# k and q of the last three spans: transposed by TensorE, or by transposing transfers on SyncE's queue

## Chip, cores and metric

The kernel runs on one NeuronCore of a Trainium2 chip. The metric is device time in microseconds of one launch; the median of three runs of the kernel before is 141.66 us (141.6 to 142.08).

## What is computed

A gated linear recurrence over 768 steps for 4 batches and 8 heads with head size 48, followed by a feed-forward layer with a maximum of two branches:

```
f = 1 / (1 + exp(-f_logit))
for t in range(S):
    state = f[:, :, t, :, None] * state + einsum('bhd,bhe->bhde', k[:, :, t], v[:, :, t])
    y[:, :, t] = einsum('bhd,bhde->bhe', q[:, :, t], state)
x = y as 3072 rows of 384 (all heads side by side)
g = maximum(x @ w1, x @ w2)        # d_ff = 1024
out = g @ w_out
```

## The kernel before

The sequence is cut into windows of 256 steps (W), and a window of one batch is a *span*: 3 windows by 4 batches make 12 spans, 0 to 11, and span s goes on from the state of span s - 4. In a span, partition p holds the two neighbouring steps 2p and 2p + 1 ("two", also called the parity), and the 128 partitions are two halves (h) of 64, each a chunk of 128 steps. The steps of a span, by their letters in the order:

- Lf, Lk, Lq, Lv (line 115) load f, k, q, v from SyncE, 384 KB each; E, F, G (ScalarE), e and C (a triangular matmul, line 261), X and Z (ScalarE) make the running sums of log f and their exponentials; i and j multiply the gates into k and q.
- K (line 291) and Q (line 294) write k and q, scaled by the exponentials, as bf16 into the padded tiles kp and qp: 128 partitions, 2 parities, 8 heads of 64 columns (48 used). There are three buffers of each. V packs v as bf16.
- t and u are the transposes: `transposes(s, 0, b)` for kp, `transposes(s, 1, b)` for qp (line 320). Each is 16 matmuls against an identity, one for each pair of heads (NP = 4), parity and half. They write bf16 into the banks b and b + 1, and U copies both banks (128 x 2048) into the tile `trs`, on ScalarE or VectorE (line 104). `trs` has three buffers.
- A (line 337, two parts) multiplies transposed k and q to the score matrix; m masks it on VectorE (line 345) into at_m. S (line 367) multiplies the state before by the transposed q; y (line 387) adds the masked scores times v. z is a short read that makes VectorE wait for y.
- D (line 401) makes the new state from k and v, n and N (lines 413, 418) add it in and scale.
- H and Y turn the result into xT, in bf16, transposed for the feed-forward layer.

The feed-forward layer of span g is d (line 445: xT by the difference w1 - w2, four parts of 12 matmuls each), r (a relu into gT, ScalarE line 452 or VectorE line 454), o (lines 460 and 463: 3 matmuls of xT with w2 w_out and 8 of gT with w_out, for each parity), b (copy out of PSUM) and O (stores, line 481, two transfers each). For the last span P, B and R do the same in halves. The letter w begins the steps that prepare the weights.

All of it is one list written out by hand, `ORDER` (lines 20 to 56): a word is a step, its span and part, its engine (a, v, p, s) and its PSUM bank. The program is issued in this order, so each engine and SyncE's queue carries out its own words in this order, and waits at a word until that word's data are there. Loads (L) and stores (O) share SyncE's queue. Toward the end of the list the loads end with Lv10, the stores O5 and O6 follow, and the transposes of spans 9, 10 and 11 stand together (u10 t9 u9 t10 t11 u11) between the d steps of spans 7 and 8 and o8.0. The products follow in the order A9, A11.0, A10, A11.1.

Of the kernel before, what the change touches and what calls it, by code (L numbers as in the profile page):

```python
# [12 lines left out]
BF16 = mybir.dt.bfloat16  # L13
# [6 lines left out]
ORDER = """  # L20
# [24 lines left out]
A7.0@0 b5.0a@7 D8@2 A7.1@3 F11a n8.0v S7@5 m7.0v@0 o6.0@7 Lk10s@10 F10a e11p G10a z7v@5 N8.0p  # L45
m7.1v@3 Lv10s@12 e10p C11@0 b6.0a@7 S8@1 i9v A8.1@3 V9p o5.1@7 z8v@1 m8.1v@3 K9v C10@3 y7 Z10a
b5.1v@7 D9@4 H7a@5 j11v y8 O5s Z11a Y7v@5 o6.1@7 X11a Q11p H8a@1 n9.0v Y8v@1 d7.0@4 b6.1a@7 i10p
G11a d7.1@5 O6s i11v d8.0@6 r7.0a@4 Q10v d8.1@7 N9.0v X10a d8.2@0 V10a K10v d8.3@1 r8.0a@6 K11v
d7.2@2 d7.3@3 r8.1v@0 u10@4 r7.1a@2 t9@6 u9@6 t10@4 t11@0 U9a@6 U10v@4 u11@0 o8.0@2 U11v@0 A9.0@3
b8.0a@2 S9@0 m9.0v@3 A9.1@6 D10@2 o7.1@5 z9v@0 m9.1v@6 V11v A11.0@3 y9 n10.0v D11@6 o7.0@2 n11.0v  # L50
m11.0v@3 N11.0p H9v@0 o8.1@3 b7.0v@2 N10.0v b7.1a@5 Y9v@0 O7s A10.0@4 b8.1a@3 S10@6 m10.0v@4
A10.1@0 d9.0@2 z10v@6 d9.1@3 m10.1v@0 d9.2@4 r9.0a@2 d9.3@5 A11.1@0 r9.1a@4 S11@2 y10 z11v@2
m11.1v@0 o9.0@4 H10a@6 Y10v@6 y11 b9.0a@4 d10.0@0 H11v@2 d10.1@1 d10.2@4 r10.0v@0 o9.1@6 Y11v@2
d10.3@5 d11.0@0 r10.1a@4 d11.1@1 b9.1a@6 d11.2@2 O9s d11.3@3 O8s o10.0@4 r11.1v@2 r11.0v@0 o10.1@3
o11.0@0 b10.0a@4 b10.1a@3 O10s P11.0@1 b11.0a@0 O11s P11.1@0 B11.0v@1 R11.0s B11.1a@0 R11.1s
"""


@with_exitstack
def kernel(  # L60
# [16 lines left out]
    C = 128  # L77
    HC = C // 2
    W = 2 * C
    nw = S // W  # L80
    NP = H // 2
# [10 lines left out]
    work = ctx.enter_context(tc.tile_pool(name="work", bufs=2))  # L92
# [8 lines left out]
    engines = {"a": nc.scalar, "v": nc.vector, "p": nc.gpsimd, "s": nc.sync}  # L101

    def copy(e, out, in_):
        (nc.scalar.copy if e == "a" else engines[e].tensor_copy)(out, in_)  # L104
# [7 lines left out]
    def load(nm, s, e, slot):  # L112
        w, b = divmod(s, B)
        src = sources[nm][b, :, w * W:(w + 1) * W, :].rearrange("h (p two) d -> p h (two d)", two=2)
        engines[e].dma_start(out=slots[:, slot, :].rearrange("p (h x) -> p h x", h=H), in_=src)  # L115
        loaded[s][nm] = slots[:, slot, :].rearrange("p (h two d) -> p h two d", h=H, two=2)

    def staged(i, a):
        return slots[:, 4 * i:4 * i + 4, :].rearrange("p s x -> p (s x)").rearrange("p (a x) -> p a x", a=a)
# [3 lines left out]
    def load_columns(dst, w, e, h):  # L123
        cols = slice(h * d_ff // 2, (h + 1) * d_ff // 2)
        engines[e].dma_start(out=dst[:, :, cols], in_=w.rearrange("(k p) m -> p k m", p=C)[:, :, cols])

    def load_wo(e, h):
        part = slice(h * FG // 2, (h + 1) * FG // 2)
        engines[e].dma_start(out=wo_f[:, part, :],
                             in_=moe_w_out.rearrange("(j p) m -> p j m", p=C)[:, part, :])  # L130
# [13 lines left out]
    for h in range(2):  # L144
        rows = slice(h * HC, (h + 1) * HC)
# [3 lines left out]
    for nm, n_bufs, shape in (("e", 2, [C, H, DP]), ("kp", 3, [C, 2, H, DP]),  # L149
                              ("qp", 3, [C, 2, H, DP]), ("vb", 4, [C, 2 * H * DP + 2 * GAP])):  # L150
        padded[nm] = []
        for i in range(n_bufs):
            t = consts.tile(shape, BF16, name=f"{nm}{i}")
# [9 lines left out]
    def pad(nm, s):  # L163
        if s not in holders[nm]:
            holders[nm].append(s)
        return padded[nm][holders[nm].index(s) % len(padded[nm])]
# [75 lines left out]
    gate, ell, one, cum, inv, dec, tr, at_b, at, states, sadd, tmps = ({} for _ in range(12))  # L242

    def step_E(s):
        gate[s] = work.tile([C, H, 2, D], F32, name="gate", tag="gate", bufs=2)
        nc.scalar.activation(flat(gate[s]), flat(loaded[s]["f"]), AF.Exp, bias=0.0, scale=-1.0)  # L246

    def step_F(s):
        ell[s] = work.tile([C, H, 2, D], F32, name="ell", tag="ell", bufs=2)
        nc.scalar.activation(flat(ell[s]), flat(gate[s]), AF.Ln, bias=1.0, scale=1.0)  # L250

    def step_G(s):
        one[s] = work.tile([C, H, D], F32, name="one", tag="one", bufs=2)
        nc.scalar.activation(one[s], ell[s][:, :, 1, :], AF.Exp, bias=0.0, scale=-1.0)

    def step_e(s, e):
        engines[e].tensor_add(pad("e", s)[:, :, 0:D], ell[s][:, :, 0, :], ell[s][:, :, 1, :])  # L257

    def step_C(s, b):
        ps, t = banks[:, b, :], pad("e", s)  # L260
        nc.tensor.matmul(out=ps[:, 0:HD].rearrange("p (h d) -> p h d", h=H), lhsT=u_inc,  # L261
                         rhs=t[:, :, 0:D], start=True, stop=True)
        for j in range(NP):
            nc.tensor.matmul(out=ps[:, HD + 2 * j:HD + 2 * j + 2],
                             lhsT=t[:, 2 * j:2 * j + 2, :].rearrange("p h e -> p (h e)"),
                             rhs=ones2, start=False, stop=True, skip_group_check=True)
        cum[s] = ps
# [56 lines left out]
    def step_U(s, e, b):  # L324
        t = work.tile([C, 2, 2, NP, 2, HC], BF16, name="trs", tag="trs", bufs=3)
        copy(e, t.rearrange("p h x j a t -> p h (x j a t)"), banks16[:, b:b + 2, :])
        tr[s] = t

    def step_A(s, jj, b):
        t = tr[s]  # L330
        for j in range(2 * jj, 2 * jj + 2):
            for par in range(2):
                for h in range(2):
                    for r in range(2):
                        rows = slice(r * DP, r * DP + D)
                        ps = banks[:, b + r, :].rearrange("p (j a t) -> p j a t", j=2, a=2)
                        nc.tensor.matmul(out=ps[h * HC:(h + 1) * HC, j % 2, par, :],  # L337
                                         lhsT=t[rows, h, 0, j, par, :],
                                         rhs=t[rows, h, 1, j].rearrange("p a t -> p (a t)"),
                                         start=True, stop=True, skip_group_check=True)  # L340

    def step_m(s, jj, b):
        if jj == 0:
            at[s] = work.tile([C, 2, 2, 2, 2, C], BF16, name="at_m", tag="at_m", bufs=2)
        nc.vector.tensor_mul(at[s][:, jj].rearrange("p r j a t -> p (r j) (a t)"),  # L345
                             banks[:, b:b + 2, :].rearrange("p r (j x) -> p (r j) x", j=2),
                             mask_f.unsqueeze(1).to_broadcast([C, 4, 2 * C]))
# [3 lines left out]
    def has_state(s, h):  # L351
        return s >= B or h > 0

    def state_before(s, h):
        return states[s][:, 0] if h else states[s - B][:, 1]

    def step_S(s, b):
        t = tr[s]
        ys[s] = [banks[:, b + h, :].rearrange("p (j t) -> p j t", j=NP) for h in range(2)]
        for h in range(2):  # L360
            if not has_state(s, h):
                continue
            st = state_before(s, h)
            for j in range(NP):
                for r in range(2):
                    rows = slice(r * DP, r * DP + D)
                    nc.tensor.matmul(  # L367
                        out=ys[s][h][r * DP:(r + 1) * DP, j, :], lhsT=st[rows, j, :],
                        rhs=t[rows, h, 1, j].rearrange("p a t -> p (a t)"),
                        start=(j == 0), stop=False, skip_group_check=True)  # L370


# [176 lines left out]
    def store_wd(part, e, b):  # L549
# [3 lines left out]

    steps = {
        "Lf": lambda s, e, b: load("f", s, e, b), "Lk": lambda s, e, b: load("k", s, e, b),
        "Lq": lambda s, e, b: load("q", s, e, b), "Lv": lambda s, e, b: load("v", s, e, b),
        "Wa": lambda i, e, b: load_columns(w1_f, moe_w1, e, i),
        "Wb": lambda i, e, b: load_columns(w2_f, moe_w2, e, i),
        "Wo": lambda h, e, b: load_wo(e, h),
        "E": lambda s, e, b: step_E(s), "F": lambda s, e, b: step_F(s), "G": lambda s, e, b: step_G(s),  # L560
        "e": lambda s, e, b: step_e(s, e), "C": lambda s, e, b: step_C(s, b),
        "X": lambda s, e, b: step_X(s), "Z": lambda s, e, b: step_Z(s),
        "i": lambda s, e, b: step_i(s, e), "j": lambda s, e, b: step_j(s, e),
        "K": lambda s, e, b: step_K(s, e), "Q": lambda s, e, b: step_Q(s, e),
        "V": lambda s, e, b: step_V(s, e),
        "t": lambda s, e, b: transposes(s, 0, b), "u": lambda s, e, b: transposes(s, 1, b),
        "U": lambda s, e, b: step_U(s, e, b),
        "A": lambda s, i, e, b: step_A(s, i, b), "m": lambda s, i, e, b: step_m(s, i, b),
        "S": lambda s, e, b: step_S(s, b), "y": lambda s, e, b: step_y(s),
        "z": lambda s, e, b: step_z(s, b),  # L570
        "H": lambda s, e, b: step_H(s, e, b), "Y": lambda s, e, b: step_Y(s, e, b),
# [9 lines left out]
        "ws": lambda i, e, b: subtract(i, e), "wp": lambda i, e, b: permuted(i, b),  # L581
        "we": lambda i, e, b: store_wd(i, e, b),
    }
    for word in ORDER.split():
        key, of, e, b = re.fullmatch(r"([A-Za-z]+)([0-9.]+)([avps]?)@?([0-9]*)", word).groups()
        steps[key](*map(int, of.split(".")), e, int(b or 0))


# [28 lines left out]
```

## Time and profile before

| | |
|---|---|
| median of three runs | 141.66 us |
| the profiled execution, device time | 142.46 us |
| its span in the trace | 140.7 us |
| granted clock of TensorE | 1.0 throughout |
| busy: TensorE matmuls / weight loads | 121.1 us (86%) / 90.0 us (64%) |
| busy: VectorE / ScalarE / GpSimd | 110.0 us (78%) / 87.5 us (62%) / 47.0 us (33%) |
| transposes, line 320, all spans | 384 matmuls, a record of one 190 ns |
| copies of trs | 7 on VectorE, mean 1218 ns; 5 on ScalarE, mean 1863 ns |
| DMA | 28.66 MB, mean 204 GB/s; no bytes to speak of from 104 to 107.4 us |

The profile is one execution. Matmuls overlap: the record of one is longer than its step, so a group's cost on the path is read from the chain of work that ended last, which follows the program back from its last instruction to what released each step. Times in all views are microseconds from the span's start. The "xN" behind a line is the number of instructions merged into it.

### The profile page before, as it was taken

To read this page: it belongs to the slowest core of one execution; us is meant where nothing else is said; L and a number is where in the kernel's file an instruction comes from. 1 tells how busy PE (TensorE), PEld (TensorE's weight loads), DVE (VectorE), ACT (ScalarE), POOL (GpSimd) and SP (SyncE) were. 2 spreads that over 40 slices of the span, in tenths; PEclk is the share of its full clock that TensorE was granted. 3 is DMA by queue.
4 is the path that set the end of the run, shared out by engine and by line. 5 is a ranking of instruction groups with operands and counts; after the bars stand their busy time and mean duration, and the time that the engine had idled before them with its cause. 6 is when DMAs were issued, how large, how long until landed. Compare 5 with 4: busy or idle time off the path is not lost.

```text
span 140.7 us, 5377 instructions
## 1 busy us (share of the span) xinstructions
PE 121.1 (86%) x2331; PEld 90.0 (64%) x2331; DVE 110.0 (78%) x196; ACT 87.5 (62%) x145; POOL 47.0 (33%) x68
## 2 busy tenths in 40 slices
PE   0033799896999999999899999997999999999990
PEld 0023679654866786868566786675886668678670
DVE  5666799896879997999979898899688895770510
ACT  3624889569988899499774999724884114303120
POOL 7444205405194536800692842529100100000000
PEclk9999999999999999999999999999999999999999
DMA  4999999999999999999999899999400012000754
GB/s 104 272 329 342 388 281 312 340 241 249 272 262 264 266 267 271 221 275 235 240 277 240 204 259 261 257 224 290 112 13 5 5 40 72 7 0 18 211 125 99
DMA packets 56248, 28.66 MB, mean 204 GB/s; under 512 B 50464, under 2 KB 54688, under 8 KB 56224
## 3 DMA queue, kind: packets, MB, share of 16 engines
q1 hardware_dynamic: 56064, 28.22, 79.3%
q8 instruction: 18, 0.29, 0.9%
q10 hardware_dynamic: 160, 0.10, 0.3%
q14 instruction: 6, 0.05, 0.1%
HBM read 23.59 MB, written 4.72 MB: 201 GB/s over the span
## 4 chain that ended last, share of the span: by engine, by line
PE 49%; DMA 13%; DVE 10%; SPq 8%; issue 6%; POOL 6%; ACT 5%; ACTq 0%; DVEq 0%; POOLq 0%
PE banks L463 16%; PE banks L445 11%; DMA slots<-in_v_dram 8%; PE banks L460 7%; SPq L115 6%; DMA slots<-in_q_dram 4%; POOL vb L104 4%; PE banks L337 4%; PE banks L320 3%; DVE wdn L536 2%; PE banks L387 2%; PE banks L367 2%; PE banks L401 2%; SPq L481 2%; DVE at_m L345 2%
## 5 line engine op out<-in xcount | busy, mean ns | idle before, releaser
L463 PE MATMUL banks<-wo,gT 128*128 128x384 bf16 x184 | 33.7, 326 | 0.0
L445 PE MATMUL banks<-xT,wd 128*128 128x256 bf16 x288 | 33.6, 273 | 0.0
L345 DVE TENSOR_TENSOR at_m<-banks,mask 128x1024 bf16<-128x1024 f32 x24 | 29.1, 1217 | 1.8 <-PE banks L337 1.6
L445 PEld LDWEIGHTS <-wd 128*128 128x128 bf16 x288 | 27.3, 98 | 3.8
L452 ACT ACTIVATE gT<-banks 128x1024 bf16<-128x1024 f32 x18 | 18.4, 1032 | 11.6 <-PE banks L445 11.4
L463 PEld LDWEIGHTS <-gT 128*128 128x128 bf16 x184 | 18.0, 98 | 11.9
L104 ACT COPY ob<-banks 128x384 f32<-128x384 f32 (+1 forms) x19 | 8.9, 468 | 20.1 <-PE banks L463 15.2
L433 DVE SCALAR_TENSOR_TENSOR xT<-tail,gaps,banks 128x256 bf16<-128x256 bf16 x36 | 15.1, 474 | 0.1
L460 PE MATMUL banks<-m,xT 128*128 128x384 bf16 x69 | 15.1, 328 | 0.0
L246 ACT ACTIVATE gate<-slots 128x768 f32<-128x768 f32 x12 | 10.2, 848 | 6.9 <-DMA slots<-in_f_logit_dram 6.9
L104 POOL CAST vb<-slots 128x384 bf16<-128x384 f32 (+2 forms) x15 | 8.7, 614 | 14.2 <-DMA slots<-in_v_dram 14.2
L257 POOL TENSOR_TENSOR e<-ell 128x384 bf16<-128x384 f32 x8 | 8.0, 1001 | 13.5 <-ACT ell L250 13.5
L337 PE MATMUL banks<-trs 48*64 48x128 bf16 x384 | 10.5, 227 | 2.2 <-DVE trs L104 1.9
L418 POOL TENSOR_TENSOR state<-tmp_s,dec 128x256 bf16<-128x256 f32 x10 | 6.4, 647 | 17.8 <-DVE tmp_s L413 17.8
L261 PE MATMUL banks<-e,u_inc 128*128 128x384 bf16 x12 | 4.2, 354 | 9.1 <-DVE e L257 7.9
L454 DVE TENSOR_SCALAR gT<-banks 128x1024 bf16<-128x1024 f32 x6 | 7.2, 1219 | 4.3 <-PE banks L445 4.3
L337 PEld LDWEIGHTS <-trs 48*64 48x64 bf16 x384 | 7.5, 110 | 4.8 <-issue 2.2
L250 ACT ACTIVATE ell<-gate 128x768 f32<-128x768 f32 x12 | 10.0, 844 | 0.4
L294 POOL TENSOR_TENSOR qp<-slots,dec 128x768 bf16<-128x768 f32 x4 | 7.3, 1818 | 8.7 <-ACT inv L271 6.7
L104 ACT COPY trs<-banks 128x2048 bf16<-128x2048 bf16 x5 | 9.3, 1863 | 0.9 <-PE banks L320 0.9
L104 DVE COPY trs<-banks 128x2048 bf16<-128x2048 bf16 x7 | 8.4, 1218 | 1.5 <-PE banks L320 1.5
L291 DVE TENSOR_TENSOR kp<-slots,inv 128x768 bf16<-128x768 f32 x8 | 7.5, 954 | 1.4 <-ACT inv L271 1.2
(73 smaller groups left out, 195.2 us busy)
## 6 DMA issues: line engine op xcount, KB each, us to landing
slots<-in_f_logit_dram SPq DMA_DIRECT2D x12, 384.0 KB, 6.5
slots<-in_k_dram SPq DMA_DIRECT2D x12, 384.0 KB, 5.7
slots<-in_q_dram SPq DMA_DIRECT2D x12, 384.0 KB, 6.2
slots<-in_v_dram SPq DMA_DIRECT2D x12, 384.0 KB, 5.9
out_dram<-ob SPq DMA_DIRECT2D x22, 192.0 KB, 3.6
slots<-in_moe_w_dram SPq DMA_DIRECT2D x4, 768.0 KB, 8.4
slots<-in_moe_w_out_dram SPq DMA_DIRECT2D x2, 768.0 KB, 7.4
out_dram<-ob SPq DMA_DIRECT2D x2, 96.0 KB, 2.2
```

Source lines behind the costliest of these rows:

```text
L104: (nc.scalar.copy if e == "a" else engines[e].tensor_copy)(out, in_)
L115: engines[e].dma_start(out=slots[:, slot, :].rearrange("p (h x) -> p h x", h=H), in_=src)
L246: nc.scalar.activation(flat(gate[s]), flat(loaded[s]["f"]), AF.Exp, bias=0.0, scale=-1.0)
L250: nc.scalar.activation(flat(ell[s]), flat(gate[s]), AF.Ln, bias=1.0, scale=1.0)
L257: engines[e].tensor_add(pad("e", s)[:, :, 0:D], ell[s][:, :, 0, :], ell[s][:, :, 1, :])
L337: nc.tensor.matmul(out=ps[h * HC:(h + 1) * HC, j % 2, par, :], lhsT=t[rows, h, 0, j, par, :], rhs=t[rows, h, 1, j].rearrange("p a t -> p ( ...
L345: nc.vector.tensor_mul(at[s][:, jj].rearrange("p r j a t -> p (r j) (a t)"), banks[:, b:b + 2, :].rearrange("p r (j x) -> p (r j) x", j=2) ...
L433: engines[e].scalar_tensor_tensor(out=x[:, kt], in0=tails[s], scalar=gaps[:, kt:kt + 1], in1=ps[:, :, kt], op0=ALU.mult, op1=ALU.add)
L445: nc.tensor.matmul(out=ps[:, f, :], lhsT=wd[:, kt, ff * C:(ff + 1) * C], rhs=xT[g][:, kt, :], start=(kt == 0), stop=(kt == KT - 1))
L452: nc.scalar.activation(dst, src, AF.Relu)
L460: nc.tensor.matmul(out=ps, lhsT=xT[g][:, kt, cols], rhs=m2[:, kt, :], start=(kt == 0), stop=False)
L463: nc.tensor.matmul(out=ps, lhsT=gT[g][:, ff, cols], rhs=wo[:, ff, :], start=False, stop=(ff == FG - 1))
```

## The change

For spans 9, 10 and 11 the words t, u and U are left out of the order. In their place stand six words T on SyncE, T*s*.0 for k and T*s*.1 for q. Each is one transposing transfer of the whole padded tile (128 x 1024 bf16) from SBUF to the tile `trs` in SBUF. T9.1 and T9.0 stand behind O6; T11.1, T10.1, T10.0 and T11.0 behind K11, still ahead of all later stores. Apart from these words the order is the same. The tile of these spans is laid out by tensor, parity, pair of heads, half and step, where U's is by half, tensor, pair, parity and step; A and S read both through the same view. `FIRST` is an empty list and does nothing.

```diff
-G11a d7.1@5 O6s i11v d8.0@6 r7.0a@4 Q10v d8.1@7 N9.0v X10a d8.2@0 V10a K10v d8.3@1 r8.0a@6 K11v
-d7.2@2 d7.3@3 r8.1v@0 u10@4 r7.1a@2 t9@6 u9@6 t10@4 t11@0 U9a@6 U10v@4 u11@0 o8.0@2 U11v@0 A9.0@3
-b8.0a@2 S9@0 m9.0v@3 A9.1@6 D10@2 ...
+G11a d7.1@5 O6s T9.1s T9.0s i11v d8.0@6 r7.0a@4 Q10v d8.1@7 N9.0v X10a d8.2@0 V10a K10v d8.3@1
+r8.0a@6 K11v T11.1s T10.1s T10.0s T11.0s d7.2@2 d7.3@3 r8.1v@0 r7.1a@2 o8.0@2 A9.0@3 b8.0a@2 S9@0
+m9.0v@3 A9.1@6 D10@2 ...
...
     def step_U(s, e, b):
         t = work.tile([C, 2, 2, NP, 2, HC], BF16, name="trs", tag="trs", bufs=3)
         copy(e, t.rearrange("p h x j a t -> p h (x j a t)"), banks16[:, b:b + 2, :])
-        tr[s] = t
+        tr[s] = t.rearrange("p h x j a t -> p x h j a t")
+
+    def step_T(s, x, e):
+        if s not in tr:
+            t = work.tile([C, 2, 2, NP, 2, HC], BF16, name="trs", tag="trs", bufs=3)
+            tr[s] = t.rearrange("p h x j a t -> p (h x j a t)").rearrange(
+                "p (x a j h t) -> p x h j a t", x=2, a=2, j=NP, h=2)
+        out = tr[s][:, x].rearrange("p h j a t -> p a j h t").rearrange("p a j h t -> p (a j) (h t)")
+        engines[e].dma_start_transpose(
+            out=out, in_=pad("kpqp"[2 * x:2 * x + 2], s).rearrange("p two h e -> p (two h e)"))
...
-                                         lhsT=t[rows, h, 0, j, par, :],
-                                         rhs=t[rows, h, 1, j].rearrange("p a t -> p (a t)"),
+                                         lhsT=t[rows, 0, h, j, par, :],
+                                         rhs=t[rows, 1, h, j],
...
-                        rhs=t[rows, h, 1, j].rearrange("p a t -> p (a t)"),
+                        rhs=t[rows, 1, h, j],
...
+        "T": lambda s, x, e, b: step_T(s, x, e),
```

More of the change, by code (lines that the diff above doesn't have):

```diff
@@ L47, with words @@
 b5.1v@7 D9@4 H7a@5 j11v y8 O5s Z11a Y7v@5 o6.1@7 X11a Q11p H8a@1 n9.0v Y8v@1 d7.0@4 b6.1a@7 i10p
-G11a d7.1@5 O6s i11v d8.0@6 r7.0a@4 Q10v d8.1@7 N9.0v X10a d8.2@0 V10a K10v d8.3@1 r8.0a@6 K11v
-d7.2@2 d7.3@3 r8.1v@0 u10@4 r7.1a@2 t9@6 u9@6 t10@4 t11@0 U9a@6 U10v@4 u11@0 o8.0@2 U11v@0 A9.0@3
[L50 to L55, printed above, removed]
-"""
+G11a d7.1@5 O6s T9.1s T9.0s i11v d8.0@6 r7.0a@4 Q10v d8.1@7 N9.0v X10a d8.2@0 V10a K10v d8.3@1
+r8.0a@6 K11v T11.1s T10.1s T10.0s T11.0s d7.2@2 d7.3@3 r8.1v@0 r7.1a@2 o8.0@2 A9.0@3 b8.0a@2 S9@0
+m9.0v@3 A9.1@6 D10@2 o7.1@5 z9v@0 m9.1v@6 V11v A11.0@3 y9 n10.0v D11@6 o7.0@2 n11.0v m11.0v@3
+N11.0p H9v@0 o8.1@3 b7.0v@2 N10.0v b7.1a@5 Y9v@0 O7s A10.0@4 b8.1a@3 S10@6 m10.0v@4 A10.1@0 d9.0@2
+z10v@6 d9.1@3 m10.1v@0 d9.2@4 r9.0a@2 d9.3@5 A11.1@0 r9.1a@4 S11@2 y10 z11v@2 m11.1v@0 o9.0@4
+H10a@6 Y10v@6 y11 b9.0a@4 d10.0@0 H11v@2 d10.1@1 d10.2@4 r10.0v@0 o9.1@6 Y11v@2 d10.3@5 d11.0@0
+r10.1a@4 d11.1@1 b9.1a@6 d11.2@2 O9s d11.3@3 O8s o10.0@4 r11.1v@2 r11.0v@0 o10.1@3 o11.0@0
+b10.0a@4 b10.1a@3 O10s P11.0@1 b11.0a@0 O11s P11.1@0 B11.0v@1 R11.0s B11.1a@0 R11.1s
+"""
+FIRST = ""
+def words(order):
+    for word in order.split():
+        key, of, e, b = re.fullmatch(r"([A-Za-z]+)([0-9.]+)([avps]?)@?([0-9]*)", word).groups()
+        yield key, tuple(map(int, of.split("."))), e, int(b or 0)
 @with_exitstack
@@ L116, in load @@
         loaded[s][nm] = slots[:, slot, :].rearrange("p (h two d) -> p h two d", h=H, two=2)
+    for key, of, e, b in words(FIRST):
+        load(key[1], *of, e, b)
     def staged(i, a):
@@ L583 @@
     }
-    for word in ORDER.split():
-        key, of, e, b = re.fullmatch(r"([A-Za-z]+)([0-9.]+)([avps]?)@?([0-9]*)", word).groups()
-        steps[key](*map(int, of.split(".")), e, int(b or 0))
+    for key, of, e, b in words(ORDER):
+        steps[key](*of, e, b)
 _INS = ['q', 'k', 'v', 'f_logit', 'moe_w1', 'moe_w2', 'moe_w_out']
```

## The prediction, made before the changed kernel was run

> **What bounds the kernel now.** I read three views in this order: the page's slices, the chain of work that ended last, and the busy time by stage. The slices show which engine is full where the change lies; one slice is 3.52 us, so 100 us is the 29th.
>
> ```profile
> PE   0033799896999999999899999997999999999990
> ...
> DVE  5666799896879997999979898899688895770510
> ACT  3624889569988899499774999724884114303120
> ...
> DMA  4999999999999999999999899999400012000754
> ```
>
> TensorE is full from the tenth slice on. VectorE is nearly as full up to the 26th, and the DMA engines are busy until the 28th: up to about 98 us several things bound together. Then the loads end, and only TensorE stays full. The chain from there, in order of time (start, length, what):
>
> ```profile
> 98.74 5.24 PE banks L445 x48
> 103.98 1.51 PE banks L320 x96
> 105.49 0.59 PE banks L460 x3
> 106.08 1.30 PE banks L463 x8
> 107.38 0.35 PE banks L337 x16
> ...
> 110.53 0.35 PE banks L337 x16
> ...
> 115.26 0.35 PE banks L337 x16
> ```
>
> L320 is the transposes: 96 of them in one block, 1.51 us, all on the chain. The three L337 lines are the first products of spans 9, 11 and 10 (A9.0, A11.0, A10.0, in this order): who needs the transposed tiles, and when. The stages (PE, PEld, DVE, ACT, POOL busy, clock, DMA share, GB/s) confirm that nothing else ends late here:
>
> ```profile
> 98.70:104.00 5.30, 5.30 (x55) 4.57 (x54) 4.18 (x6) 4.13 (x8) 0.18 (x1) 1.00 0.33 80
> 104.00:105.50 1.50, 1.50 (x97) 1.45 (x97) 0.98 (x2) 1.48 (x2) 0.00 (x0) 1.00 0.00 0
> 105.50:107.40 1.90, 1.90 (x18) 1.00 (x22) 1.90 (x2) 1.30 (x1) 0.00 (x0) 1.00 0.00 0
> 107.40:115.30 7.90, 7.90 (x169) 5.30 (x173) 7.06 (x16) 0.96 (x3) 0.62 (x1) 1.00 0.02 4
> 115.30:136.10 20.80, 20.80 (x284) 15.77 (x281) 10.33 (x16) 6.21 (x10) 0.00 (x0) 1.00 0.27 67
> ```
>
> TensorE has no gap from 98.7 to 136.1, so each microsecond taken from it here reaches the end, and each microsecond of waiting put into it does too. The DMA engines are idle from 104 to 107.4.
>
> [...] after the 7.9 us of idling at the start, 32 products of L337 took 1.07 us, later 0.64.
>
> ```profile
> 14.86 1.07 PE L337 MATMUL banks<-trs 48*64 48x128 bf16 x32 [1.64 <-DVE trs L104]
> 27.51 0.64 PE L337 MATMUL banks<-trs 48*64 48x128 bf16 x32 [0.31 <-DVE trs L104]
> ```
>
> **Removed on TensorE.** Spans 9, 10, 11, two tensors, 16 transposes each: 96, the block above: -1.51 us on the chain. (Each record shows 190 ns, but they overlap to 15.7 ns per step, so a price by the single record would be twelve times too high.) What is late next: o8.0 moves from 105.49 to 103.98. It reads in its last four products what the DVE relu r8.1 writes, and that ends at 103.33 + 1.22 = 104.55; at 0.59 us for its first three products and 1.30/8 for each later one, the first of the last four starts at 103.98 + 0.59 + 4 x 0.163 = 105.22. It fits with 0.67 us to spare.
>
> **Removed copies.** One on ScalarE (1.86 us) and two on VectorE (2.36 us together), at 105 to 107.4. They stand beside the matmuls L460 and L463 and not on the chain: nothing. If TensorE stopped being the bound, they would give back at most those 2.36 us. The PSUM banks of the transposes come free earlier, which no chain entry waits for.
>
> **Changed reads.** The tile of these spans has another layout: the moving operand of A and S is two runs of 64 instead of 128 in a row. L261 reads runs of 48 with gaps and takes 326 ns for 384 columns, L460 reads 384 in a row in 330: nothing. At the worst, were each of their 144 products (32 of A and 16 of S in each span) 5 ns longer, 0.7 us.
>
> **Added on SyncE's queue.** The six transfers T9.1 T9.0 T11.1 T10.1 T10.0 T11.0 stand behind the stores of O6, the last of which issues at
>
> ```profile
> 99.93 0.60 SPq L481 DMA_DIRECT2D out_dram<-ob  x1
> ```
>
> so SyncE is free at 100.53. The sources are ready or nearly: K9, Q9 and Q11 are written by 97.92 (the last by POOL, from 96.10, 1.82), the others by VectorE:
>
> ```profile
> 100.19 0.95 DVE L294 TENSOR_TENSOR qp<-slots,dec 128x768 bf16<-128x768 f32 x1
> ...
> 101.58 1.83 DVE L291 TENSOR_TENSOR kp<-slots,inv 128x768 bf16<-128x768 f32 x2
> ```
>
> The last at 103.41, when the sixth transfer won't yet have its turn. So the queue itself sets the time. If each transfer holds it for X and the last needs L more to land, T9 is there at 100.53 + 2X + L and T11 at 100.53 + 6X + L. They are needed 1.51 earlier than the chain shows: A9.0 at 107.38 - 1.51 = 105.87, A11.0 at 110.53 - 1.51 = 109.02. A10.0 comes 4.73 us after A11.0 and finds its tile there. TensorE takes its queue in order: what is behind a waiting A11.0 (y9, D11, o7.0, o8.1) waits too.
>
> L: no store lands in less than 1.9 us after issue, with 0.5 to 0.6 of it the issue; I take 1.5.
>
> X is the one cost that this trace doesn't show. One transfer carries 128 x 1024 bf16 = 262,144 bytes in 1,024 rows of 256 bytes[...].
> - [...]
> - By rows, from this trace: a load moves 1,024 rows of 384 bytes; at the 259 GB/s of a full stage (84 to 88.3 us) that is 1.5 us.
> - [...]
> - [...]
>
> I take 2.26[...].
>
> **The sum.** T9 lands at 100.53 + 4.52 + 1.5 = 106.55, 0.68 late. T11 lands at 100.53 + 13.56 + 1.5 = 115.59, 6.57 after 109.02; this contains the 0.68. The second wait alone is 5.89 us[...], +1.7 (between 0 and 2.3; the latter from the start of this trace, where from 14.86 to 20.58, 5.7 us, products took some 40% of their time too much). Together -1.51 + 6.57 + 1.7 = +6.8. The profiled execution took 142.46 us (span 140.7, 1.76 around it) and would take 149.3; the median of the runs shown is 0.8 lower, and on it I forecast 141.66 + 6.8 = **148.4 us**. Behind the six on SyncE wait the stores of O7, due at about 111 and now issued after 114.1: their buffer is taken again only by b11.0 at the end, over 20 us later: nothing. With copies gone from VectorE nothing else stretches.
>
> **Rivals.**
> - Faster: the transfers run at the rate of copies, in the idle DMA engines after 101. The DMA share of 0.00 from 104 to 107.4 speaks for it[...]. At X = 1.0 T9 lands at 104.0 and T11 at 108.0, both in time, and the whole block is saved: 141.66 - 1.51 = 140.15. It decides this way while 6X + 1.5 stays under 109.02 - 100.53, X under 1.17; the stall has eaten the gain at X = 1.42.
> - No change: X is about 1.5, by rows. T11 lands at 111.0, 2.0 late: +0.5, 142.2 us. For it speaks that the loads of this trace are small rows throughout; against it that these rows lie in SBUF.
> - Much slower[...]. X = 3.5 puts T11 at 123.0: -1.51 + 14.0 + 1.7 = +14.2, 155.9 us. [...]
> - Other engines as the bound: VectorE is 7.06 of 7.90 us busy in the stage from 107.4, but after the change it starts this stage 2.36 us less loaded. I give it nothing.
>
> **How the numbers follow.** Fast (X up to 1.3): 0.22. Near 1.4 to 1.5: 0.11. Likeliest (1.5 to 3.5): 0.50, on its own 142.4 to 155.9. Above: 0.17. The range goes from the full gain, 140.1, to X = 3.5, 155.9, and leaves out the last case. 0.5% is 0.7 us, about what a measurement of this kernel can tell from no change: faster 0.22, same 0.11, slower 0.67.
>
> **What would show it.** No L320 between 103.9 and 105.5. Six issues on SyncE after 100.5, each 2.2 us apart: right; 0.6 apart and landing within 3 us: the fast rival. TensorE's waits before L337 of span 11 (some 6 us) and span 9 (under 1), their releaser a DMA into trs; the L463 behind them slower than 0.163 us per step for some microseconds if the clock falls. I am wrong if A11.0 starts at about 109.0, or if the transfers take over 3.5 us each.

## The result, and the profile after

| | before | after |
|---|---|---|
| median, first set (4 runs each) | 141.63 us | 143.22 us |
| ratio, 95% interval | | 1.0107 [1.0072, 1.0143] |
| again, in a later set (43 and 22 runs) | 142.18 us | 143.06 us |
| ratio, 95% interval | | 1.0046 [1.0021, 1.0072] |
| profiled execution, device time / span | 142.46 / 140.7 us | 142.89 / 141.1 us |

Medians here and below are of all executions, while the ratios leave out those more than 1.5% above the fastest of their kernel, and so can differ from the quotient of the medians.

The change makes the kernel about 1 us slower, not 6.8. The page's slices of after, TensorE and the DMA engines, show where: the row of nines now has dents in slices 30 and 32 (the one in the 27th lies ahead of the change, as the one in the 28th did before), and the DMA engines, idle there before, are busy into the 32nd.

```profile
PE   0033899997999999999999999969969699999990
...
DMA  4999999999999999999999999889699313000844
```

The chain of work that ended last, in order of time, names the two dents:

```profile
98.27 5.25 PE banks L467 x48
...
103.54 1.03 ACT gT L474
...
104.62 0.65 PE banks L482 x3
...
106.56 0.38 PE banks L359 x16
...
107.89 3.10 DMA trs<-kp
...
111.03 0.42 PE banks L359 x16
```

The block of 96 transposes behind the 48 d matmuls is gone: 1.51 us won. But o8.0 (L482) doesn't follow at 103.52. It waits until 104.62 for ScalarE's r7.1, which reads PSUM banks 2 and 3, and o8.0 writes bank 2: 1.10 us lost. A9.0 (first L359) finds its tile. A11.0 (the L359 at 111.03) waits for the sixth transfer: TensorE's waits list 1.3 us for it, and it takes nothing from behind A11.0 meanwhile (busy 0.02 us from 109.7 to 111). Along the chain that is -1.51 + 1.10 + 1.3 = +0.9. As causes the two waits don't add up, though: A11.0 starts when the sixth transfer lands, and without the wait at o8.0 it would only wait longer there (shown below by the run with another bank). From the start of the d block to A11.0 it is 111.03 - 98.27 = 12.76 us, before 110.53 - 98.74 = 11.79: +0.97. Behind A11.0 nothing changes: A10.0 follows 4.80 us later, before 4.73.

SyncE's queue (start, length) shows the six issues:

```profile
100.14 1.48 SPq L348 DMA_TRANSPOSE trs<-qp  x1
101.68 2.01 SPq L348 DMA_TRANSPOSE trs<-kp  x1
103.79 2.62 SPq L348 DMA_TRANSPOSE trs<-qp  x2
106.50 2.68 SPq L348 DMA_TRANSPOSE trs<-kp  x2
```

The last four follow each other by 1.35 to 1.39 us, each issue 1.24 to 1.30 long, where a store takes 0.60. From issue to landing it is 3.1 to 3.4 us for these four. T9.0 lands at 105.78 and T11.0 at 110.99.

### The profile page after: what moved, and what is told of

It reads as the page before. It is cut to its first block, busy times and chain, and to the rows that moved or that the text cites. A ratio compares the mean times of both kernels' runs of the same rounds, so it can differ in the third digit from the quotient of the medians.

```text
span 141.1 us, 5192 instructions
## 1 busy us (share of the span) xinstructions
PE 120.3 (85%) x2235; PEld 89.0 (63%) x2235; DVE 108.1 (77%) x194; ACT 85.9 (61%) x144; POOL 46.8 (33%) x68
## 4 chain that ended last, share of the span: by engine, by line
PE 69%; DMA 12%; DVE 6%; POOL 5%; ACT 3%; issue 2%; SPq 1%; ACTq 0%; DVEq 0%; POOLq 0%
PE banks L467 21%; PE banks L485 18%; PE banks L482 8%; DMA slots<-in_f_logit_dram 5%; PE banks L359 5%; DMA slots<-in_v_dram 4%; PE banks L409 4%; PE banks L332 3%; POOL vb L113 3%; PE banks L389 2%; PE banks L423 2%; DVE at_m L367 2%; DMA trs<-kp 2%; PE banks L566 2%; PE banks L273 1%
## 5 line engine op out<-in xcount | busy, mean ns | idle before, releaser
L482 PE MATMUL banks<-m,xT 128*128 128x384 bf16 x69 | 15.1, 327 | 1.1 <-ACT gT L474 1.1
L359 PE MATMUL banks<-trs 48*64 48x128 bf16 x384 | 10.5, 227 | 3.3 <-DVE trs L113 2.0
L113 POOL CAST vb<-slots 128x384 bf16<-128x384 f32 (+2 forms) x15 | 8.0, 571 | 14.3 <-DMA slots<-in_v_dram 14.3
L359 PEld LDWEIGHTS <-trs 48*64 48x64 bf16 x384 | 7.5, 110 | 5.9 <-DVE trs L113 2.2
L303 POOL TENSOR_TENSOR kp<-slots,inv 128x768 bf16<-128x768 f32 x4 | 7.5, 1864 | 4.1 <-DVE slots L292 4.0
L435 DVE TENSOR_TENSOR tmp_s<-banks,state 128x256 f32<-128x256 f32 x16 | 6.7, 418 | 2.7 <-PE banks L423 2.3
```

Of the source, the lines that this page charges most:

```text
L303: engines[e].tensor_mul(pad("kp", s)[:, :, :, 0:D], by_parity(loaded[s]["k"]), both(inv[s]))
L482: nc.tensor.matmul(out=ps, lhsT=xT[g][:, kt, cols], rhs=m2[:, kt, :], start=(kt == 0), stop=False)
```

## The experiments

The measure below, beside the median, is the stretch from the start of the d block to A11.0, read from each profile's chain as above (for the plain copies and merged, from TensorE's timeline). It leaves out what differs upstream from run to run: the start of the block alone lies between 97.8 and 98.8 us in all these profiles but halves (99.5). The runs come from three sets on different chips, each with its own runs of the kernel before, which is why that median changes from row to row; between sets the stretch and the ratio are the better guides.

| kernel | d block to A11.0 (us), against before | median / median of before | ratio, 95% |
|---|---|---|---|
| changed, again | 12.80, +1.01 | 143.06 / 142.18 | 1.0046 [1.0021, 1.0072] |
| bank | 12.52, +0.73 | 144.10 / 142.18 | 1.0118 [1.0065, 1.0171] |
| bank again | 12.63, +0.84 | 144.26 / 142.14 | 1.0093 [1.0058, 1.0128] |
| order | 11.46, -0.33 | 141.78 / 142.18 | 0.9970 [0.9945, 0.9994] |
| bank and order | 10.73, -1.06 | 140.84 / 142.18 | 0.9900 [0.9860, 0.9940] |
| early | 10.19, -1.60 | 140.18 / 142.21 | 0.9871 [0.9823, 0.9918] |
| early, bank 2 | 11.45, -0.34 | 141.53 / 142.14 | 0.9969 [0.9949, 0.9990] |
| merged | 10.98, -0.81 | 141.28 / 142.14 | 0.9931 [0.9905, 0.9957] |
| plain copies | 11.88, +0.09 | 141.75 / 142.21 | 0.9971 [0.9945, 0.9996] |
| a seventh | 14.36, +2.57 | 146.31 / 142.21 | 1.0272 [1.0199, 1.0344] |
| halves | 20.53, +8.74 | 153.56 / 142.21 | 1.0725 [1.0638, 1.0811] |

**The changed kernel again.**

> The changed kernel once more, on the chip of the next three. My theory: against the chain of before it loses 1.10 us where o8.0 waits for PSUM bank 2 (ScalarE relu r7.1a still reads it) and 1.47 us where A11.0 waits for the sixth transfer, and wins 1.51 us for the 96 transposes: +1.06 us, about 142.7 beside a kernel before of 141.6. Rival: a part of the slowdown (the medians differ by 1.6 us) comes from somewhere else, so the ratio is again about 1.011 while both waits are the same length as in the first trace.

Both waits are as long as at first, but the ratio is 1.0046, not 1.011 (the two intervals just meet, at 1.0072): the rival falls. The stretch says +1.0 us, this median +0.9. What the first set of four runs had beyond that didn't come again, and where it came from is not known.

**The bank alone.**

```diff
-r7.1a@2 o8.0@2 A9.0@3 b8.0a@2
+r7.1a@2 o8.0@5 A9.0@3 b8.0a@5
```

> o8.0 and its copy b8.0 use PSUM bank 5 in place of bank 2. My theory: o8.0 starts right behind the last d, 1.1 us earlier, but A11.0 then waits so much longer for the sixth transfer, which lands at the same time: 0.0 us against the changed kernel (within 0.3). Rival: the bank wait is what costs, and the end comes 1.1 us earlier.

By the trace as expected: o8.0 follows at once, TensorE then waits for transfers twice (A9.0 0.3 to 0.5 us, A11.0 1.8 to 2.1 us, over this run and its repeat), and A11.0 again starts when the sixth transfer lands:

```profile
108.09 3.13 DMA trs<-kp
...
111.27 0.42 PE banks L359 x16
```

The stretch is only 0.2 us shorter (T9.0's issue took 1.75 us in the repeat, 2.01 in the changed kernel). So in the changed kernel the bank wait costs next to nothing: the sixth transfer sets the time. But the median is 1 us *above* the changed kernel, which neither theory had. The same kernel was therefore run once more:

> The bank edit alone once more, for a narrower interval. My theory: the time of the changed kernel, 0.7 to 1.1 us over the kernel before, since A11.0 waits for the sixth transfer whatever TensorE does ahead of it. Rival (the edit itself costs something, as its median of 144.1 us could mean): 1.7 us or more over the kernel before.

The median came out high again. The granted clock of the single executions tells them apart. In 9 of these 19 its mean is 0.993 or more, and their median is 143.03 us: the changed kernel's 143.02 (20 of its 22 executions). In the other 10 it is 0.985 to 0.988, and their median is 144.6. So the edit itself costs nothing where the clock holds. That the longer pause at A11.0, 1.8 to 2.1 us instead of 1.3, more often lets the clock fall is argued from these counts, as neither profile of this kernel caught a fall; the difference, 1.6 us, is about what one fall costs under the seventh transfer, where it was caught (1.5).

**The order of the transfers.**

```diff
-T11.1s T10.1s T10.0s T11.0s
+T11.1s T11.0s T10.1s T10.0s
```

> T11.0 moved ahead of T10.1 and T10.0, nothing else. My theory: span 11's tile lands as the fourth transfer, at about 108.4, A11.0 finds it there, and 1.4 us of waiting goes; A10.0 comes after 114 and finds its tile too: -1.4 us against the changed kernel, 0.4 under the kernel before. Rival (the wait at A11.0 only shows what another limit behind it would take anyway, such as VectorE or the later stores): under 0.5 us faster than the changed kernel.

-1.3 us in both measures, against the changed kernel. The chain has no transfer left from the d block on:

```profile
98.53 5.25 PE banks L467 x48
...
103.81 1.03 ACT gT L474
...
106.83 0.35 PE banks L359 x16
...
109.99 0.35 PE banks L359 x16
```

The wait at A11.0 was real, and only the place in the queue made it. What is left of the 1.51 us is 1.51 - 1.10 = 0.4.

**Both.** The edits of bank and of order together.

> Both edits. My theory: with the sixth transfer out of the way the bank now counts, but A9.0 then meets the second transfer, which lands at about 105.8, 0.4 after it could start: -1.4 - 0.7 = -2.1 us against the changed kernel, some 1.1 under the kernel before (140.5 beside 141.6). Rival (the two waits are independent and each is worth what it shows): -2.5 us. Rival (the bank is worth nothing at all): -1.4 us.

-2.2 us against the changed kernel by the medians, -2.1 by the stretch; expected -2.1. A9.0 now waits 0.5 us for the second transfer, which lands at 106.06. So the bank, worth almost nothing alone, is worth 0.7 by the stretch once the sixth transfer is out of the way.

**Span 9's transfers earlier.** On top of both:

```diff
-O5s Z11a
+O5s T9.1s T9.0s Z11a
...
-O6s T9.1s T9.0s i11v
+O6s i11v
```

> As bank_order, and T9.1 and T9.0 moved ahead of the stores of O6, right behind those of O5. My theory: span 9's tile lands before 102 and A9.0 no longer waits for it, so the whole block of 1.51 us is saved: another 0.7 us under bank_order, about 1.5 under the kernel before (140.6 beside a before of 142.2). Rival: there the transfers meet the last load (v of span 10), V10 comes late and holds up r7.0 behind it on ScalarE; then nothing is gained or up to 1 us lost. The issue of T9.0 shows the price of issuing alone: about 1.25 us if issuing sets the rate, about 0.6 if the DMA engines do.

The fastest of all versions, 1.3% under the kernel before. The chain runs through on TensorE alone:

```profile
98.22 5.24 PE banks L467 x48
103.46 0.49 PE banks L482 x3
103.95 1.30 PE banks L485 x8
105.25 0.35 PE banks L359 x16
...
108.41 0.35 PE banks L359 x16
```

The stretch is 1.60 us shorter than before: the whole block of 1.51, and 0.10 because the first three products of o8.0 take 0.49 us right behind the d block, where they took 0.59 behind the transposes. The transfers met no load that mattered: TensorE waits for none of them. T9.1 issues at 96.0 and takes 1.38 us, T9.0 1.55: nearer the expectation's 1.25 than its 0.6, but not a clean price, as the DMA engines were busy (share 1.09 from 98.2 to 103.4 us).

**The same, with o8.0 in bank 2.** Against the version before it:

```diff
-r7.1a@2 o8.0@5 A9.0@3 b8.0a@5
+r7.1a@2 o8.0@2 A9.0@3 b8.0a@2
```

> As early, but o8.0 and b8.0 back in bank 2: the two transfers of span 9 early and T11.0 fourth, nothing else. My theory: no wait for a transfer is left, so the bank wait now counts in full: 1.1 us over early, 1.51 - 1.10 = 0.4 us under the kernel before, the same as order, where span 9 was in time as well. Rival (the bank wait only counts together with a late transfer): the time of early, 1.5 us or more under the kernel before.

It gives the stretch of order (11.45 and 11.46) and its median within 0.3 us. The bank wait counts in full as soon as no transfer is late: 1.26 us in the stretch, 1.10 of waiting and 0.16 because the first three products behind it take 0.65 us, not 0.49.

**What sets 1.36 us: halves.** Each transfer cut into two of 128 x 512:

```diff
+        for a in range(2):
+            engines[e].dma_start_transpose(
+                out=out[:, a * NP:(a + 1) * NP, :], in_=src[:, a].rearrange("p h e -> p (h e)"))
```

> Each of the six transfers cut into two of half the size, nothing else. My theory (the DMA engines are full and set 1.36 us for each 256 KB; issuing is held up by them): the same bytes take the same time, T11.0 lands within 0.5 us of where it did, and the time is that of the changed kernel within 0.5 us. Rival (issuing sets the rate[...]): a half takes 1.0 us of SyncE, the twelve end 2.8 us later, +2.8 us.

Both fell, the theory wholly, and the loss is far more than the rival's 2.8 us. SyncE's queue, twelve issues now:

```profile
101.36 4.30 SPq L350 DMA_TRANSPOSE trs<-qp  x2
105.72 2.56 SPq L350 DMA_TRANSPOSE trs<-kp  x2
108.39 5.13 SPq L350 DMA_TRANSPOSE trs<-qp  x4
113.62 5.14 SPq L350 DMA_TRANSPOSE trs<-kp  x4
```

Half the bytes in half the rows, and an issue still takes 1.20 to 1.27 us, where a whole one took 1.24 to 1.30. The stages (second-last number: DMA share) show that the engines don't hold it up:

```profile
105.00:110.00 5.00, 2.65 (x37) 1.54 (x38) 0.29 (x1) 1.26 (x2) 0.00 (x0) 1.00 0.48 96
```

So issuing a transposing transfer costs some 1.25 us of SyncE at 128 x 512 and at 128 x 1024. A price of the issue that grows with the size, on which the prediction rested, is refuted here: half the size changes it by less than 0.1 us. Of the 10.5 us over the changed kernel the stretch explains 7.8, six issues more; behind its pauses TensorE also runs at a lower clock (mean 0.966 to 0.974 in all four executions).

**Plain copies.** The six transfers without transposing; the target's rows are 144 elements apart, so that the pieces stay 256 bytes:

```diff
-            out=out, in_=pad("kpqp"[2 * x:2 * x + 2], s).rearrange("p two h e -> p (two h e)"))
...
+            t = work.tile([C, 2, 2 * NP, C + 16], BF16, name="trs", tag="trs", bufs=3)
...
+        engines[e].dma_start(
+            out=plains[s][:, x, :, 0:C],
+            in_=pad("kpqp"[2 * x:2 * x + 2], s).rearrange("p two (j r) e -> p (two j) (r e)", r=2))
```

> The six transfers are plain copies of the same bytes in the same 1,024 pieces of 256 bytes each; k and q of spans 9 to 11 are left untransposed, so part of the computation is left out. My theory (the transposing costs nothing beyond moving 1,024 small rows): SyncE's issues follow each other by 1.2 to 1.4 us as before and the wait at A11.0 stays within 0.5 us of 1.5. Rival [...]: issues follow by 0.6 to 1.1 us, the sixth lands 2 us earlier and A11.0 doesn't wait: 1.5 us under the changed kernel.

In between. A plain issue can take 0.62 us, half of a transposing one:

```profile
99.70 0.63 SPq L350 DMA_DIRECT2D trs<-qp  x1
100.38 0.85 SPq L350 DMA_DIRECT2D trs<-kp  x1
101.33 3.10 SPq L350 DMA_DIRECT2D trs<-qp  x2
104.53 1.90 SPq L350 DMA_DIRECT2D trs<-kp  x2
```

Yet the sixth lands 9.95 us after the first issue (at 109.65), in the changed kernel 10.85 (110.99). From 104.5 to 109.5 the engines are full (share 0.96) and move 206 GB/s, in the changed kernel from 104 to 110 also full (1.08) and 212 (from 104 to 109 us in 4,365 packets for 1.08 MB, some 250 bytes each). That is 262,144 bytes in 1.24 to 1.27 us: the engines have a limit of their own for such pieces, and it happens to lie at the same 1.25 us as the issue. Without transposing the sixth lands 0.9 us sooner, not 2.

**One transfer per span.** kp and qp in one tile, three transfers (T9.0, T11.0, T10.0) of 512 KB, with the edits of bank and order.

```diff
+        kq.append(consts.tile([C, 2, 2, H, DP], BF16, name=f"kq{i}"))
+    padded["kp"], padded["qp"] = [t[:, 0] for t in kq], [t[:, 1] for t in kq]
...
+        engines[e].dma_start_transpose(
+            out=whole[s].rearrange("p (b t) -> p b t", t=C),
+            in_=kq[at_s].rearrange("p x two h e -> p (x two h e)"))
```

> kp and qp of a span lie side by side in one tile, so that each span is one transposing transfer of 512 KB: T9, T11, T10, with the bank edit. If an issue costs 1.25 us whatever its size and nothing else limits: three issues of about 1.3 us, T11 lands near 106, A9.0 finds its tile, and the time is that of early. If the 16 DMA engines limit (1.25 us for each 1,024 pieces of 256 bytes, as in plain): the issues stretch to about 2.5 us, T9 lands at 105.5 to 106 as in bank_order and T11 at 108.4, and the time is that of bank_order, 0.5 to 0.7 us over early. [...]

The second case, the engines' limit. T9 waits long behind the stores, the other two read:

```profile
103.99 1.91 SPq L357 DMA_TRANSPOSE trs<-kq  x1
105.98 2.18 SPq L357 DMA_TRANSPOSE trs<-kq  x1
```

They land at 108.4 and 110.8: 2.4 us for 512 KB, so again 1.2 for 256 KB. The stretch is 0.25 us longer than with bank and order. Half as many issues bring nothing, because the engines were already full (from 104 to 110 us they move 224 GB/s, in the changed kernel 212).

**A seventh transfer.** One more ahead of T11.0, into a tile that nobody reads.

```diff
-K11v T11.1s T10.1s T10.0s T11.0s
+K11v T11.1s T10.1s T10.0s M10.0s T11.0s
```

> One more transposing transfer (k of span 10 again, into a tile that nobody reads) ahead of T11.0. My theory: T11.0 lands one interval later and A11.0 waits 1.2 to 1.4 us longer: +1.3 us against the changed kernel. Rival (the wait at A11.0 isn't set by the place in the queue): under 0.4 us.

Against the changed kernel the stretch is 1.6 us longer (1.42 of it one more interval: T11.0 issues at 109.62, 1.42 after the transfer ahead of it). The median rose by 3.25. The stages (TensorE busy first, granted clock third from the end) show the other half:

```profile
109.80:112.90 3.10, 0.19 (x2) 0.00 (x1) 0.87 (x4) 0.48 (x1) 0.00 (x0) 0.99 0.79 148
112.90:117.40 4.50, 4.50 (x76) 3.21 (x77) 1.89 (x3) 0.00 (x0) 0.62 (x1) 0.63 0.02 4
117.40:120.00 2.60, 2.60 (x58) 1.74 (x57) 2.39 (x6) 0.48 (x1) 0.00 (x0) 1.00 0.24 51
```

After 2.9 us of waiting the granted clock is 0.63 over the next 4.5 us (the 32 products of y9 take 1.07 us by record, in the changed kernel 0.62), and 1.00 again from 117.4. A11.0, y9, D11 and o7.0 take 112.90 to 117.42 where the changed kernel takes 111.03 to 114.04: 4.52 against 3.01, +1.5 us.

## Why the prediction was wrong, by its steps

- **The bound and the gain.** Right. From 98.7 us TensorE alone sets the end, the block is worth 1.51 us, and early gets it back whole (-1.60 in the stretch). The copies and the changed reads were worth nothing, as said: 16 products of A take 0.42 us by record in both layouts.
- **"It fits with 0.67 us to spare."** Wrong, and missed by asking only what o8.0 *reads*. It also writes PSUM bank 2, which r7.1 on ScalarE still read until 104.57. The transposes had covered that wait, and the trace of before had it to read: r7.1 ended there at 104.02 + 1.02 = 105.04, 1.06 us behind the 103.98 at which the prediction started o8.0.

```profile
104.02 1.02 ACT L452 ACTIVATE gT<-banks 128x1024 bf16<-128x1024 f32 x1 [0.70 <-PE banks L445]
```

In the changed kernel this miss cost next to nothing (bank, -0.2 in the stretch). It counts once the transfers are in time: bank and order against order alone, -0.73; early against early with bank 2, -1.26.
- **"I take 2.26."** This is the step that failed: the mechanism, a queue of six whose last holds up A11.0, was right, but its price was not. X is 1.36 us, so 6 x 0.90 = 5.4 us of the forecast delay never came, and with it the slower clock that hung on the long wait. 2.26 was my estimate, a price of the issue that grows with the size, which no trace had shown; measured, the issue is some 1.25 us, at half the size too. And the 16 engines needed 1.2 to 1.27 us for 256 KB in pieces of 256 bytes, transposed or not. The estimate by rows from this trace's own loads, 1.5, was the nearest, and I had passed over it. Transposing ran at nearly the rate of copying (10.85 against 9.95 us for the six), and with the engines full that rate was 206 to 212 GB/s.
- **L.** 1.5 was low: from the end of the issue to the landing of T11.0 it was 110.99 - 109.19 = 1.8.
- **The queue as the cause of the wait.** Right: with T11.0 fourth, no wait for a transfer is left (order), with one more ahead the wait grows by 1.6 us, 1.42 of it one interval (seventh). With X = 1.36 and L = 1.8 the prediction's own formula gives T11 at 100.14 + 8.16 + 1.8 = 110.1. It landed 0.9 later, because the issues of the first two were longer, 1.48 and 2.01 us; why is open.
- **The clock, +1.7.** The trace gave only its upper end, 2.3, and that was read too high: at 19.23 us the 32 products of y already take 0.64, later 0.62. The 1.7 itself was my estimate. It wasn't due: the pause is 1.3 us, not 5.9, and behind it the clock reads 1.0 and A11.0's 16 products take 0.42 us by record, as before. Where the pause is 2.9 us (seventh) the slower clock comes, 0.63 over 4.5 us, and costs 1.5, near the forecast 1.7.
- **The sign** came out as forecast, but partly by luck. From +6.8, take 5.4 for X and 1.7 for the clock, and add 0.3 for L and 0.9 for the longer first issues: about +0.9, where +0.97 was measured. The right X alone would have put the forecast at a small gain (-1.51 + 1.17 = -0.3); the sign came from the first issues, which I had not.
- **Another reading of the trace** was off, without effect: TensorE is full from the eleventh slice on, not the tenth (a 6).

## What to carry to other kernels

Before taking work off an engine, list for the instruction behind it every release it needs, buffers that it writes as well as data that it reads: removed work may have hidden a wait (here 1.10 us behind 1.51 us of work). A row of transfers on one queue has the order of its deadlines: here moving one word was worth 1.3 us, and moving two more ahead of a store another 0.5 to 0.7. For an unknown transfer, begin with the rate of the same kernel's transfers of like pieces (here 1.5 us by the loads, 1.36 measured).

## What I had not expected of the hardware

- A transposing issue held SyncE for 1.25 us at 128 x 512 and at 128 x 1024 alike; a store's or a plain copy's can take 0.60 to 0.63. At 128 x 2048 it was 1.91 and 2.18, with the engines full; how much of that is the issue's own stays open.
- The first transposing transfers behind stores had longer issues: 1.48 and 2.01 us in the changed kernel, 4.30 for the first two together in halves, 3.69 for the first in merged. In the changed kernel the engines were nearly idle from 103 to 103.5 us (share 0.14) while T9.0's issue still ran. Plain copies show a hold of this kind too (3.10 us for the third and fourth together). What it waits for was not settled.
- Pauses of TensorE of 1.3 to 2.9 us went with a lower clock in some executions. Where the profile shows a pause of 1.3 us (the changed kernel), the mean clock was below 0.993 in 2 of 26 executions, at 1.8 to 2.1 us (bank) in 13 of 25, at 2.9 us (seventh) in 3 of 4; where no pause behind the d block is over 1.1 us (order, and early with bank 2) in none of 44. Of these, only the fall behind the 2.9 us was itself profiled.
- The granted clock doesn't show every slowing: from 14 to 20 us of the kernel before it reads 1.00 too, though 32 products take 1.07 us there and 0.64 later (lines in the prediction).
